# Windowed attention and mixture of experts on one core: the product with v as two runs of equal shapes, with constants, router groups and gate products moved

## The chip, the core and the metric

The kernel runs on one core of a Trainium2 chip. The core has a matrix engine (TensorE; PE in the profile, PEld for its weight loads), a vector engine (VectorE, DVE), an activation engine (ScalarE, ACT), a general engine (GpSimd, POOL) and a queue engine (SyncE, SP) that here only issues transfers. The engines run on their own and wait for one another through semaphores. Sixteen DMA engines carry the transfers of all queues. The metric is the device time of one execution in microseconds; the median of the runs shown stands for a kernel.

## The reference

Two stages, cut to what is computed. The first is causal attention with a window of 64 positions, for 8 batches, 8 heads, 576 positions and head size 64; the second sends each of the 4608 rows that passes a skip test to the best of 8 experts.

```python
scores = np.matmul(q, k.transpose(0, 1, 3, 2)) / np.sqrt(D)
rel = pos[:, None] - pos[None, :]
scores = np.where((rel >= 0) & (rel < 64), scores, -1e9)
attn = np.exp(scores - scores.max(-1)); attn /= attn.sum(-1) + 1e-9
x = (attn @ v)                                   # 4608 rows of 512
do_compute = x @ w_skip > 0
xc = x[do_compute]; logits = xc @ w_gate; e_idx = argmax(logits)
gate_w = softmax(logits)[e_idx]
h = np.maximum(xc[e_idx == e] @ w1[e], 0)        # per expert e
out[do_compute] = xc + gate_w * (h @ w2[e])
```

## The kernel before, in words

**Attention tiles.** A block is 64 positions of one batch. A tile `t` holds two blocks, 128 rows of x; there are 36. In 32 of them the two blocks follow each other in one batch; in the other four (tiles 8, 17, 26 and 35) they are the last blocks of two batches. A block attends to itself and to the block ahead of it, so a tile of the first kind needs three blocks of k and v, and the middle one is shared by both halves.

**One tile, step by step.** `score` (L244) writes the raw scores of a tile to `ps` in PSUM. `soften` selects the window (DVE, L260), takes the row maximum (DVE, L263), scales it (ACT, L264) and takes eight exponentials into `s` (ACT, L267). `transpose_p` turns `s` over on PE into two buffers `pt` (L276); ACT copies the first to `pm` (L283, L287), POOL multiplies that with the mask into `ptm` (L284, L288), and DVE does the rest of the mask (L291, the function that `transpose_p` returns and the loop calls as `masks`). `gate` and `gate_t` make the router's products with v ahead of time: `pw` on PE (L326), its copy `vw` on ACT (L328), `pk` on PE (L339), and the copy of that into columns 65 to 73 of `vm` on ACT (L340). `pt`, `pw`, `pk` and later `px` and `p1` share one tag `t` of two PSUM buffers in rotation. `av_tile` multiplies `ptm` with `vm` on PE into `av` (L376, one buffer), and DVE divides by the row sums into `x` and `lh` (L386 to L394).

**The product with v.** Four pairs of heads `q` and two halves `z` of the partitions give, for a tile with a shared block, eight products of 64 rows by 128 columns of weights (the middle block, for both halves of the tile at once) and sixteen of 64 by 64. The program writes 24 matmuls; the chip runs each float32 matmul as two instructions, so the profile counts 48 for a tile. The loop stands over `q`, and inside it come first the products of the shared block and then the others of the same `q`.

**The order of the work.** The instructions of every engine stand in the order in which the program issues them. Step `t` of the loop at the end of the program issues `score(t + 1)`, the gate products, `transpose_p(t)`, a step of the router, `soften(t + 1)`, loads, `masks`, `tile_out(t - 1)` (that is `av_tile`) and more router steps.

**The router.** `GRP` cuts the 36 tiles into groups. When the last tile of a group is out, `route` starts for the group: a generator of some 16 small DVE instructions (L421 to L482), an exponential on ACT, and sums on PE (L449, L452) that go into a free part of `av`. Each call of `routes(1)` runs it to its next `yield`. Its results are list entries, one POOL scatter for each tile (`scatter`, L528), of which `pace(1)` issues one. When 22 tiles are out (`NCLOSE`), the lists of the two fullest experts are closed (`close_first`), read back (`first_lists`, `es`), and four gathers fetch the first expert rows (`gather_x`, L551, `xg`). In steps `XSPLIT` the first two of them are turned over on PE into `px` (L739). In steps `U0` one 512 KB load of expert weights each is issued (`weight_dma_first`); in a step of `USPLIT` the first piece is split into a high and a low part (`weight_split`: ACT L702, DVE L703).

**The experts.** Behind the loop the last two tiles are interleaved with expert work (`p`, L750 to L752, and so on), which fills the rest of the program.

**Constants.** Nine small loads stand on ACT's queue ahead of its first instruction; the last three are those of `load_constants`.

## Time and profile before

| | |
|---|---|
| three runs | 497.98, 493.5 and 498.54 us, median 497.98 |
| the profiled execution | 500.87 us; span from its first to its last instruction 499.2 us |
| busy share of the span | PE 90%, PEld 73%, DVE 57%, ACT 42%, POOL 36% |
| first product with v (tile 0) starts | 19.96 us |
| product of tile 14 starts | 88.12 us |
| product of tile 34 starts, and first expert matmul | 219.49 us, 223.87 us |
| mean granted TensorE clock | 0.934 of full speed |

Busy PE is not PE at its peak: matmuls overlap in the engine, and their ends are modelled. How long a stage takes is read from the starts of its instructions. [...]

### The profile page before, as it was taken

How to read it: one execution, taken by the hardware profiler on the slowest of the kernel's cores; microseconds unless marked ns; L12 is line 12 of the kernel's file. 1: busy time of each engine (PE TensorE's matmuls, PEld its weight loads, DVE VectorE, ACT ScalarE, POOL GpSimd, SP SyncE). 2: the span in 40 equal slices, each digit the busy share in tenths (PEclk: the TensorE clock that was granted, in tenths of full speed). 3: DMA queues.
4: the chain of work that ended last, by engine and by line, in shares of the span. 5: the costliest groups of instructions: out<-in, count | busy, mean ns of one | idle time of the engine just before them, and what ended most of it. 6: DMA issues, size and time to landing. Idle time of an engine off the chain costs nothing.

```text
span 499.2 us, 12731 instructions
## 1 busy us (share of the span) xinstructions
PE 451.2 (90%) x5001; PEld 365.7 (73%) x5001; DVE 283.0 (57%) x600; ACT 211.3 (42%) x604; POOL 178.5 (36%) x213
## 2 busy tenths in 40 slices
PE   3999999899988994988798999999999999999990
PEld 3677767666765773767797988898888889888770
DVE  2356665665666664457963364967437456666420
ACT  1665665444434452334731252443424435543410
POOL 4343443344644546336525351420604313101010
PEclk9999999898977897668899999999999999999996
DMA  8879998868877698316743455364645655656000
GB/s 306 334 226 298 301 298 256 313 176 275 224 257 213 181 356 301 110 44 201 260 121 142 165 186 167 121 245 149 205 161 173 204 180 183 224 194 207 3 26 18
DMA packets 34958, 99.90 MB, mean 200 GB/s; under 512 B 6092, under 2 KB 7910, under 8 KB 34888
## 3 DMA queue, kind: packets, MB, share of 16 engines
q1 hardware_dynamic: 28864, 88.52, 54.5%
q0 software_dynamic: 4864, 9.90, 5.9%
q8 instruction: 40, 0.66, 0.5%
q10 hardware_dynamic: 1168, 0.65, 0.4%
q14 instruction: 22, 0.18, 0.1%
HBM read 84.82 MB, written 14.94 MB: 200 GB/s over the span
## 4 chain that ended last, share of the span: by engine, by line
PE 76%; DVE 8%; DMA 6%; issue 3%; ACT 3%; another core or an unknown queue 0%; POOLq 0%; SPq 0%; ACTq 0%; DVEq 0%
PE av L376 17%; PE p L750 7%; PE p L751 7%; PE p L752 7%; PE ps L244 5%; PE pt L276 5%; PE yw L750 3%; PE yv L750 3%; PE yw L751 3%; PE yv L751 3%; PE yw L752 3%; PE yv L752 3%; DMA raw<-wq 3%; PE px L739 2%; PE pk L339 2%
## 5 line engine op out<-in xcount | busy, mean ns | idle before, releaser
L376 PE MATMUL av<-vm,ptm 64*64 64x74 f32 (+1 forms) x1536 | 101.5, 285 | 1.9 <-DVE lh L394 1.5
L703 DVE TENSOR_TENSOR wlo<-raw,whi 128x1024 fp32r<-128x1024 f32 x72 | 87.8, 1222 | 14.3 <-ACT whi L702 12.4
L376 PEld LDWEIGHTS av<-vm,ptm 64*64 64x64 f32 (+1 forms) x1536 | 75.2, 164 | 27.6 <-issue 9.3
L787 ACT ACTIVATE hh<-p 128x256 fp32r<-128x256 f32 (+6 forms) x72 | 27.7, 385 | 140.6 <-PE p L752 139.2
L750 PE MATMUL p<-xh,whi 128*128 128x256 f32 (+6 forms) x288 | 85.8, 298 | 1.1 <-DVE hl L788 1.1
L751 PE MATMUL p<-xl,whi 128*128 128x256 f32 (+6 forms) x288 | 84.7, 294 | 0.0
L752 PE MATMUL p<-xh,wlo 128*128 128x256 f32 (+6 forms) x288 | 84.5, 293 | 0.0
L702 ACT CAST whi<-raw 128x1024 fp32r<-128x1024 f32 x72 | 74.5, 1046 | 0.0
L284 POOL TENSOR_TENSOR ptm<-pm,mask 128x512 f32<-128x512 f32 x36 | 45.9, 1276 | 76.1 <-ACT pm L283 76.0
L788 DVE SCALAR_TENSOR_TENSOR hl<-p,hh 128x256 fp32r<-128x256 f32 (+6 forms) x72 | 30.3, 420 | 70.3 <-ACT hh L787 64.6
L267 ACT ACTIVATE s<-ps,nmx 128x64 f32<-128x64 f32 x288 | 63.0, 330 | 1.2
L810 POOL DMA_INDIRECT out<-yo,les x18 | 19.0, 1054 | 122.3 <-DVE yo L809 109.8
L750 PEld LDWEIGHTS p<-xh,whi 128*128 128x128 f32 x288 | 55.7, 193 | 4.0 <-DVE hl L788 1.2
L528 POOL DMA_INDIRECT lists<-ent,gdi x36 | 40.7, 1130 | 46.4 <-DVE lh L394 22.6
L751 PEld LDWEIGHTS p<-xl,whi 128*128 128x128 f32 x288 | 55.8, 194 | 1.4
L752 PEld LDWEIGHTS p<-xh,wlo 128*128 128x128 f32 x288 | 55.7, 194 | 0.0
L276 PE MATMUL pt<-ident,s 128*128 128x128 f32 x144 | 34.5, 328 | 13.1 <-ACT vw L328 6.3
L386 DVE TENSOR_SCALAR r<-av 128x8 f32<-128x8 f32 x36 | 6.0, 166 | 71.1 <-PE av L376 69.4
L244 PE MATMUL ps<-k,q 64*64 64x128 f32 (+1 forms) x1024 | 42.7, 295 | 0.8 <-issue 0.8
L276 PEld LDWEIGHTS pt<-ident,s 128*128 128x128 f32 x144 | 16.3, 153 | 30.7 <-ACT vw L328 11.3
L244 PEld LDWEIGHTS ps<-k,q 64*64 64x64 f32 x1024 | 34.8, 153 | 2.0 <-issue 1.8
L750 PE MATMUL yw<-whi,hh 128*128 128x512 f32 x80 | 32.3, 403 | 0.0
(171 smaller groups left out, 703.2 us busy)
## 6 DMA issues: line engine op xcount, KB each, us to landing
raw<-wq SPq DMA_DIRECT2D x72, 512.0 KB
vm<-vp SPq DMA_DIRECT2D x16, 592.0 KB
vT<-vT SPq DMA_DIRECT2D x16, 512.0 KB
out<-x SPq DMA_DIRECT2D x32, 256.0 KB
q<-qT SPq DMA_DIRECT2D x14, 512.0 KB
k<-kT SPq DMA_DIRECT2D x7, 640.0 KB
k<-kT SPq DMA_DIRECT2D x7, 512.0 KB
kt<-kT SPq DMA_DIRECT2D x8, 256.0 KB
```

What stands on the lines that cost most here:

```text
L244: nc.tensor.matmul(ps[64 * hf : 64 * hf + 64, z, p, 64 * w.start :], q[h, p], k[h, w, p], start=True, stop=True, skip_group_check=True,)
L267: nc.scalar.activation(s[:, q, z], cur[:, z, q], AF.Exp, bias=nmx[:, z, q : q + 1], scale=0.125)
L276: nc.tensor.transpose(pt[:, i], s[:, 2 * g + i].rearrange("p z c -> p (z c)"), ident)
L284: nc.gpsimd.tensor_tensor(part(0, 2), split(pm[:, 0:2], 2), kept(2), op=ALU.mult)
L376: nc.tensor.matmul(av[64 * f0 : 64 * f1, z, q * VW : (q + 1) * VW], ptm[h, q, j : j + f1 - f0], v[h, q], start=first, stop=not first or (f ...
L528: ins = nc.gpsimd.indirect_dma_start(out=lists, out_offset=bass.IndirectOffsetOnAxis(ap=di, axis=0), in_=ent.bitcast(I32), in_offset=None, ...
L702: nc.scalar.copy(hi, raw)
L703: nc.vector.tensor_tensor(lo, raw, hi.bitcast(F32), op=ALU.subtract)
L750: nc.tensor.matmul(o, lh, rh, start=first, stop=False)
L751: nc.tensor.matmul(o, lh, rl, start=False, stop=False)
L752: nc.tensor.matmul(o, ll, rh, start=False, stop=last)
L788: beat(nc.vector.scalar_tensor_tensor(hl[:, f], p1, 0.0, hh[:, f].bitcast(F32), op0=ALU.max, op1=ALU.subtract))
```

## The change

The product with v loops over the shapes first and over `q` inside: all products of the shared block, then all others; the flags that open and close the sums follow that. In a tile without a shared block both kinds are 64 by 64. The gate products stand behind the transposes of the same step. The router's steps stand behind `soften` and the first feed of loads, ahead of `masks` and behind it. `GRP` has six groups instead of five: 8, 8, 6, 8, 4 and 2 tiles. `load_constants` moves from ACT's queue to SP's and into step 1 of the loop, ACT's other loads are put in another order, and `onesb` gets its ones early, followed by one exponential of zero times itself (its values stay one). `U0`, `USPLIT`, `XSPLIT` and `TWICE` go up by one; the loop ends with step 34, so that no step of it is in `USPLIT` any more.

```diff
-U0 = (28, 29, 30, 31, 32, 33)
-USPLIT = (34,)
+U0 = (29, 30, 31, 32, 33, 34)
+USPLIT = (35,)
-XSPLIT = (32, 33)
+XSPLIT = (33, 34)
-TWICE = 20
+TWICE = 21
...
     def load_constants():
-        nc.scalar.dma_start(cf, a["c_f"])
-        nc.scalar.dma_start(trib, a["c_tri"])
-        nc.scalar.dma_start(
+        nc.sync.dma_start(cf, a["c_f"])
+        nc.sync.dma_start(trib, a["c_tri"])
+        nc.sync.dma_start(
...
-        nc.gpsimd.memset(onesb, 1.0)
         nc.gpsimd.tensor_copy(base, cf[:, off["base"]])
...
-        for q in range(4):
-            parts = [] if shared else [(hf, hf + 1, 2 * hf + 1, win[hf][0], True) for hf in range(2)]
-            if shared:
-                parts.append((0, 2, 1, win[0][0], True))
-            parts += [
-                (0, 1, 0, win[0][1], False),
-                (1, 2, 3 if shared else 2, win[1][0] if shared else win[1][1], False),
-            ]
-            for n, (f0, f1, j, v, first) in enumerate(parts):
...
+        if shared:
+            both = [(0, 2, 1, win[0][0])]
+            rest = [(0, 1, 0, win[0][1]), (1, 2, 3, win[1][0])]
+        else:
+            both = [(hf, hf + 1, 2 * hf + 1, win[hf][0]) for hf in range(2)]
+            rest = [(hf, hf + 1, 2 * hf, win[hf][1]) for hf in range(2)]
+        for parts in (both, rest):
+            for q in range(4):
+                for f0, f1, j, v in parts:
...
-    GRP = [14, 8, 8, 4, 2]
+    GRP = [8, 8, 6, 8, 4, 2]
...
         load_qk(0, 0, 2)
+        nc.scalar.dma_start(band, a["c_band"])
         nc.scalar.dma_start(identb, a["c_identb"])
-        nc.scalar.dma_start(band, a["c_band"])
         nc.scalar.dma_start(sel, a["c_sel"])
+        nc.scalar.dma_start(wg, a["wg"])
         nc.scalar.dma_start(ident, a["c_ident"])
         nc.scalar.dma_start(mask, a["c_mask"])
-        nc.scalar.dma_start(wg, a["wg"])
+        nc.gpsimd.memset(onesb, 1.0)
+        nc.scalar.activation(onesb, onesb, AF.Exp, scale=0.0)
...
-        load_constants()
...
             score(t + 1)
+            masks = transpose_p(t)
             for f, n in gate_at.get(t, ()):
                 f(n)
-            masks = transpose_p(t)
             rest = its[0].split(*xhl[0], XSPLIT.index(t), "t") if t in XSPLIT else None
-            routes(1)
             soften(t + 1)
             pace(1)
             feed(t, 0)
+            if t == 1:
+                load_constants()
+            routes(1)
             masks()
+            routes(1)
             if t >= 1:
                 tile_out(t - 1)
...
             if rest is not None:
                 rest()
-            routes(1)
             routes(1 if t < NCLOSE - 1 else 2)
```

On PE, step 2 of the loop stands so before; `ps` are scores, `pk` a gate product, `pt` transposes and `av` the product of tile 1:

```order
L244 MATMUL ps<-k_108,q 64x128 x16
L339 MATMUL pk<-ident,vw_301 64x64 x8
L276 MATMUL pt<-ident,s 128x128 x4
L376 MATMUL av<-vm,ptm 128x74 x2
L376 MATMUL av<-vm,ptm 64x74 x4
L376 MATMUL av<-vm,ptm 128x74 x2
L376 MATMUL av<-vm,ptm 64x74 x4
L376 MATMUL av<-vm,ptm 128x74 x2
L376 MATMUL av<-vm,ptm 64x74 x4
L376 MATMUL av<-vm,ptm 128x74 x2
L376 MATMUL av<-vm,ptm 64x74 x4
```

The eight runs of the product become two, and the gate product stands behind the transposes. The same step on PE, after:

```order
L243 MATMUL ps<-k_108,q 64x128 x16
L275 MATMUL pt<-ident,s 128x128 x4
L338 MATMUL pk<-ident,vw_310 64x64 x8
L375 MATMUL av<-vm,ptm 128x74 x8
L375 MATMUL av<-vm,ptm 64x74 x16
```

The number of matmuls is the same; the row length that order prints first is that of the output's partitions.

On DVE, the first router group ends before with tile 13; its steps stand there between that tile's `lh` and the window (`ps`) and maximum (`mx`) of tile 16, in one piece:

```order
L394 TENSOR_TENSOR lh<-av,r 128x8x9
L421 TENSOR_REDUCE lg<-lh 128x126
L428 TENSOR_REDUCE gmx<-lg 128x14
L430 TENSOR_TENSOR gd<-lg,gmx 128x112
L433 SCALAR_TENSOR_TENSOR gfi<-gd,cf 128x112
L435 TENSOR_REDUCE gfm<-gfi 128x14
L260 COPY_PREDICATED ps<-sel,ps 128x8x64
L263 TENSOR_REDUCE mx<-ps 128x8
```

The first group now ends with tile 7, and on DVE its steps stand so:

```order
L393 TENSOR_TENSOR lh<-av,r 128x8x9
L420 TENSOR_REDUCE lg<-lh 128x72
L259 COPY_PREDICATED ps<-sel,ps 128x8x64
L262 TENSOR_REDUCE mx<-ps 128x8
L427 TENSOR_REDUCE gmx<-lg 128x8
L429 TENSOR_TENSOR gd<-lg,gmx 128x64
L290 TENSOR_TENSOR ptm<-pt,mask 128x256
L432 SCALAR_TENSOR_TENSOR gfi<-gd,cf 128x64
L434 TENSOR_REDUCE gfm<-gfi 128x8
```

One router instruction instead of five stands ahead of the next tile's window and maximum, and the rest behind them.

On POOL, the four gathers of the first expert rows stand before among the mask products (`ptm`) of tiles 31 and 32; `es` are the list entries they go by:

```order
L607 TENSOR_TENSOR es_115<-es_115,ok_116 128x4
L608 TENSOR_TENSOR es_115<-es_115,ok_116 128x4
L551 DMA xg_117<-out,es_115 128x512
L284 TENSOR_TENSOR ptm<-pm,mask 128x512
L288 TENSOR_TENSOR ptm<-pm,mask 128x256
L551 DMA xg_118<-out,es_115 128x512
L551 DMA xg_119<-out,es_115 128x512
L284 TENSOR_TENSOR ptm<-pm,mask 128x512
L288 TENSOR_TENSOR ptm<-pm,mask 128x256
L551 DMA xg_120<-out,es_115 128x512
```

The first gather stands there behind the mask product of tile 30, and PE turns its rows over in step 32. After, the mask products in the piece are those of tiles 29 and 30:

```order
L606 TENSOR_TENSOR es_115<-es_115,ok_116 128x4
L607 TENSOR_TENSOR es_115<-es_115,ok_116 128x4
L283 TENSOR_TENSOR ptm<-pm,mask 128x512
L287 TENSOR_TENSOR ptm<-pm,mask 128x256
L550 DMA xg_117<-out,es_115 128x512
L550 DMA xg_118<-out,es_115 128x512
L283 TENSOR_TENSOR ptm<-pm,mask 128x512
L287 TENSOR_TENSOR ptm<-pm,mask 128x256
L550 DMA xg_119<-out,es_115 128x512
L550 DMA xg_120<-out,es_115 128x512
```

The first gather stands behind the mask product of tile 29, and PE turns its rows over in step 33.

## Rows read from the trace of the kernel before

**Rows 1.** The page: busy time, share of the span and instructions of each engine; and the granted TensorE clock in 40 slices of the span, in tenths.

```profile
PE 451.2 (90%) x5001; PEld 365.7 (73%) x5001; DVE 283.0 (57%) x600; ACT 211.3 (42%) x604; POOL 178.5 (36%) x213
...
PEclk9999999898977897668899999999999999999996
```

**Rows 2.** Busy time of each engine in four stretches: from the product of tile 0 to that of tile 14, from there to that of tile 34, the handover to the experts, and the experts. Columns: stretch, its length, busy time and instructions of each engine, granted clock, busy share of the DMA engines, GB/s.

```profile
19.96:88.12 68.16, 66.84 (x1311) 49.56 (x1310) 40.35 (x97) 40.47 (x169) 27.37 (x28) 1.00 0.87 276
88.12:219.49 131.37, 113.46 (x1902) 84.20 (x1902) 78.57 (x212) 57.36 (x237) 63.56 (x68) 0.83 0.72 228
219.49:260.00 40.51, 35.72 (x299) 31.86 (x300) 32.54 (x86) 17.84 (x29) 19.07 (x19) 0.85 0.53 170
260.00:499.20 239.20, 223.79 (x1355) 192.29 (x1353) 127.00 (x200) 88.68 (x145) 61.23 (x80) 0.98 0.47 157
```

**Rows 3.** PE in order of time: the first product with v, one whole tile of the quiet stretch, tile 14, and the handover to the experts. Columns: start, length, engine, line, what, count, idle time before it.

```profile
19.96 2.78 PE L376 MATMUL av<-vm,ptm 64*128 64x74 f32 x30
...
32.48 1.05 PE L244 MATMUL ps<-k,q 64*64 64x128 f32 x32
33.35 0.64 PE L339 MATMUL pk<-ident,vw 64*64 64x64 f32 x16
33.92 0.88 PE L276 MATMUL pt<-ident,s 128*128 128x128 f32 x4
34.74 2.73 PE L376 MATMUL av<-vm,ptm 64*128 64x74 f32 x48
...
88.12 2.73 PE L376 MATMUL av<-vm,ptm 64*128 64x74 f32 x48
...
219.49 4.45 PE L376 MATMUL av<-vm,ptm 64*128 64x74 f32 x48 [1.53 <-DVE lh L394]
223.87 0.58 PE L750 MATMUL p<-xh,whi 128*128 128x256 f32 x1
```

**Rows 4.** PE in order of time, in short windows inside the product of tile 2 (a shared block; the first two instructions of a pair of heads, the second two, the first four 64-by-64 ones, and the second two of the next pair) and of tile 8 (no shared block).

```profile
29.92 0.34 PE L376 MATMUL av<-vm,ptm 64*128 64x74 f32 x2
30.09 0.28 PE L376 MATMUL av<-vm,ptm 64*128 64x74 f32 x2
30.30 0.29 PE L376 MATMUL av<-vm,ptm 64*64 64x74 f32 x4
30.76 0.28 PE L376 MATMUL av<-vm,ptm 64*128 64x74 f32 x2
...
59.33 0.36 PE L376 MATMUL av<-vt,ptm 64*64 64x74 f32 x8
59.51 0.31 PE L376 MATMUL av<-vm,ptm 64*64 64x74 f32 x8
59.63 0.31 PE L376 MATMUL av<-vt,ptm 64*64 64x74 f32 x8
```

**Rows 5.** The start, in order of time: the first row maximum on DVE, the first gate product on PE with its wait for a constant, ACT's table load, the first exponentials, and the first transpose on PE.

```profile
7.70 0.69 DVE L263 TENSOR_REDUCE mx<-ps 128x8 f32<-128x512 f32 x1
...
10.04 1.08 PE L326 MATMUL pw<-vT,wg 128*32 128x256 f32 x8 [1.42 <-DMA wg<-wg]
10.78 1.28 ACT L264 ACT_TABLE_LOAD   x1 [10.78 <-DMA cf<-c_f]
...
12.31 1.75 ACT L267 ACTIVATE s<-ps,nmx 128x64 f32<-128x64 f32 x8
12.88 0.48 PE L276 MATMUL pt<-ident,s 128*128 128x128 f32 x1 [1.76 <-ACT s L267]
```

**Rows 6.** A quiet tile, in order of time: DVE takes up a finished product, and the exponentials of the scores that PE makes meanwhile.

```profile
66.44 0.17 DVE L386 TENSOR_SCALAR r<-av 128x8 f32<-128x8 f32 x1 [1.83 <-PE av L376]
...
69.35 1.75 ACT L267 ACTIVATE s<-ps,nmx 128x64 f32<-128x64 f32 x8
```

**Rows 7.** The end of the first router group, in order of time: the first of its instructions on DVE, the window of the next tile behind them, ACT's wait for the maximum, and the products of the two tiles after that on PE.

```profile
87.45 1.20 DVE L421 TENSOR_REDUCE lg<-lh 128x126 f32<-128x1008 f32 x1
...
90.62 0.69 DVE L260 COPY_PREDICATED ps<-sel,ps 128x512 f32<-128x512 int32 x1
...
92.06 0.21 ACT L264 ACTIVATE nmx<-mx 128x8 f32<-128x8 f32 x1 [3.57 <-DVE mx L263]
...
95.29 4.35 PE L376 MATMUL av<-vm,ptm 64*128 64x74 f32 x48
...
103.44 2.73 PE L376 MATMUL av<-vm,ptm 64*128 64x74 f32 x48
```

**Rows 8.** The first gather of expert rows, as POOL issues it, and the transposes on PE that wait for it.

```profile
191.51 1.10 POOL L551 DMA_INDIRECT xg<-out,es  x1 [0.92 <-DMA qt<-qT]
...
197.65 1.09 PE L739 MATMUL px<-ident,xg 128*128 128x128 f32 x4 [5.76 <-DMA xg<-out,es]
```

**Rows 9.** Two of the stretches at half clock (columns as in rows 2).

```profile
95.43:102.26 6.83, 6.83 (x90) 4.72 (x90) 2.59 (x12) 1.92 (x9) 1.70 (x4) 0.50 0.73 267
194.41:208.07 13.66, 10.35 (x101) 8.35 (x101) 4.15 (x16) 3.37 (x13) 6.66 (x9) 0.50 0.53 182
```

**Rows 10.** The first splits of expert weights: two high parts on ACT, and the first low part on DVE.

```profile
216.16 2.04 ACT L702 CAST whi<-raw 128x1024 fp32r<-128x1024 f32 x2
...
220.64 1.22 DVE L703 TENSOR_TENSOR wlo<-raw,whi 128x1024 fp32r<-128x1024 f32 x1
```

**Rows 11.** The stretch in which the loads of the start fill the DMA engines (columns as in rows 2).

```profile
5.00:20.00 15.00, 11.22 (x140) 7.58 (x138) 4.59 (x7) 6.94 (x25) 2.96 (x7) 1.00 1.02 381
```

## The prediction, made before the result was known

> **What bounds the kernel now.** I read the page's first part and the clock line, then a table by stage, then PE in order of time, and last what stands around PE's waits. PE is busy for 90% of the span [rows 1], so the question is what of that is work. The table [rows 2] cuts the span: 20 us of start, 68 us for 14 tiles, 131 us for the next 20, 40 us of handover, 239 us of experts. Nothing that the change edits runs in the last stage (223.79 of 239.20 us busy at a clock of 0.98), so I leave it alone.

> In the quiet stretch a tile takes 68.16 / 14 = 4.87 us, and PE has next to no gap. Per tile the others are busy for 40.35 / 14 = 2.88 us (DVE), 2.89 (ACT) and 1.96 (POOL), and the DMA engines for 0.87 x 4.87 = 4.24 us, at 276 GB/s, which is 1.34 MB a tile [rows 2]. PE is the bound, and 2.7 us of its 4.87 are the product with v [rows 3].

> Inside that product the time goes to something other than arithmetic. A pair of heads takes 30.76 - 30.09 = 0.67 us: 0.17 from the first two 64-by-128 instructions to the second two, 0.21 from there to the first 64-by-64 ones, and 0.29 for these and the way back [rows 4]. In tile 8, where all instructions are 64 by 64, a batch of eight follows the one ahead of it after 0.12 to 0.13 us, and only the first batch takes 0.18 [rows 4]. So a run of one shape settles at 0.065 us for four instructions, its first step costs 0.05 more, and the turns between shapes cost the rest. That the second product adds onto the first in PSUM isn't the price: in tile 8 it does so too.

> In the later stretch 20 tiles take 131.37 us, 34 more than 20 x 4.87. There PE waits, and the clock falls to half behind the waits: 0.83 on average [rows 2].

> **The product with v.** Before, a shared tile is 4 x 0.67 = 2.67 us. After, it is one run of eight 64-by-128 passes, a turn, and one run of eight 64-by-64 passes. The unknown is how closely 64-by-128 passes follow when they no longer stop. The first step is 0.17; in the 64-by-64 run the later steps are 0.05 shorter than the first, and I take the same: 0.12. That gives 0.17 + 6 x 0.12 = 0.89, the turn 0.21, the second run 0.115 + 6 x 0.065 = 0.51, and the way out 0.17: 1.78 us, **0.89 us less**. Bounds: if no step gets shorter, 7 x 0.17 + 0.21 + 7 x 0.115 + 0.17 = 2.38 (0.29 less); if the wide passes follow as closely as the narrow ones, 1.45 (1.22 less). No loss is possible from the same instructions with fewer turns, save through other engines. Tiles 8, 17, 26 and 35 gain nothing, but they are short already.

> [...]

> So a quiet tile is 4.87 - 0.89 = **3.98 us** of PE. Then other things come close. DMA: 1.34 MB at the 381 GB/s of the start [rows 11] is 3.5 us; at 276 / 0.87 = 317 GB/s it is 4.2. The loop through softening: from DVE's taking up of a product to the end of the exponentials of the scores made behind it are 71.10 - 66.44 = 4.66 us [rows 6]; the transposes that need them come a tile later, so two tiles must hold those 4.66 us, half the transposes (0.44), the gate product (0.6) and one product with v (1.8): 7.5 us, or 3.75 a tile. DVE and ACT at 2.9 are further off. I take 3.98.

> **The gate products behind the transposes** cost nothing: the same work in another place, with the copy of `pt` (0.4 us on ACT) covered by the second transposes; if that cover goes, some 0.3 us a tile come back. They also take away waits of the transposes for the copy of the gate product, which I leave out.

> **The router.** At the end of the first group its five instructions hold DVE from 87.45 to 90.62, ACT waits 3.57 us, and PE starts tile 15 7.2 us after tile 14 and tile 16 another 8.15 later, at half clock [rows 3, 7]. Now one instruction, for 8 tiles instead of 14, stands ahead of the next window. There is one group more, but each step holds at most 1.6 us of such work, which fits into DVE's 3.98 - 2.88 = 1.1 us of slack but for half a microsecond. The same holds for the closing of the lists in steps 25 to 28. Of the 34 us of excess I give 17 us to these bursts and the slow clock behind them, and leave 6.

> **The gathers.** The first gather is issued at 191.51, and PE waits 5.76 us for it [rows 8], after which the clock stays at half until 208.07 [rows 9]. Now the gather stands two steps further ahead of its transposes, and a tile ahead of where it stood: at 4 us a tile, 12 us or more for a transfer of 6. That wait goes, with the slow clock about 10 us; the two sets of transposes (1.1 us each) stay.

> What remains of the 34 us: 6 for bursts, 2 for the transposes, 4 for stalls that I see no edit for, and 4 for DMA, since 3 MB of weights now have to come within six tiles that are each 0.9 us shorter. That makes **16 us**.

> **The start.** The three loads of `load_constants` keep ACT from its table load until 10.78; that takes 1.28 us, and exponentials start at 12.31, though the maximum was there at 8.39 [rows 5]. Without those loads, and with the table loaded early, they start near 8.7. What is late next are the last of ACT's other constants (the sixth, then `wg`, was waited for until 10.04 [rows 5]; now it is `mask`, with `ident` ahead of it) and PE's own work for the first two tiles, so that of the 3.6 us I count **2.5**; between 1 and 3.6. `cf` and the lists move to SP's queue; behind them wait loads of step 1 (`q`, `vT`), needed four tiles later.

> **The handover.** No split of a weight piece is left in the loop. Before, the first low part is done by 221.9, and expert matmuls start as soon as tile 34 is out [rows 3, 10]. Now it stands on DVE behind the division of tile 34 (1.35 us) and takes 1.22: **2.6 us** of PE waiting. Between 1.2 (only DVE's work) and 4.

> **Sum**, against the profiled execution (500.87 us). From the product of tile 0 to that of tile 34: before 199.5 us; after 34 x 3.98 + 16 = 151.3: 48.2 less. Start 2.5 less, the product of tile 34 itself (4.4 at half clock) 1.5 less, handover 2.6 more: 49.6 less, 451.3 us. The profiled execution lies 2.9 us above the median of the runs, so the forecast is **449 us**.

> **Rivals.** (a) Another engine takes over: DMA or softening holds a tile at 4.4 us, and stalls stay at 25. Then 34 x 4.4 + 25 = 174.6, 25 less instead of 48: 472 us. For it: DMA's 0.87 share and both bounds within 0.5 us. Against: at the start the same engines carry 381 GB/s [rows 11].
> (b) The change doesn't do what it says: passes of one shape don't close up (0.29 a tile). Then 34 x 4.58 + 16 = 171.7, 28 less from there: 470 us; with nothing at all from the product, 480. Against: tile 8.
> (c) Slower: the clock. It fell whenever PE waited: behind the router at 95.43, during the wait for the gather at 194.41 [rows 9]; at half clock tile 15 took 103.44 - 95.29 = 8.15 us [rows 7], and with the shorter product 4.35 x 0.89 / 2.67 = 1.45 less, 6.7. A PE that waits in every tile could stay there. Before, a tile took 199.5 / 34 = 5.87 on average; it decides from (5.87 - 3.98) / (6.7 - 3.98) = 69% of the tiles at half clock. At 85% a tile is 6.3: 214, 15 us more, 512 us. [...] Against: at 3.98 us a tile PE is still the last to finish, and in the quiet stretch, with no gaps, the clock stayed at 1.00 [rows 2].

> **How the numbers follow.** The forecast's own case (435 to 462) has 0.70, (a) 0.15, (b) 0.07, (c) 0.04; 0.04 is left for things unseen on either side. The price of the product (0.29 to 1.22 less) is the widest term: at its best end, 34 x 0.33 = 11 us below, tempered by DMA and softening; at the other, (b). The range 432 to 476 holds the forecast's case, (a) and most of (b). Within 1%, which is what a measurement here can tell from no change, lies little of any case: faster 0.93, same 0.03, slower 0.04.

> **What would show it.** In the profile after: the product of a shared tile at 1.5 to 1.9 us at full clock, in two runs; quiet tiles of 3.8 to 4.3 us; no wait of `px` for a gather; the first product at 17 to 18 us; tile 34 at 165 to 175 us; expert matmuls some 2.6 us behind tile 34; and the same 239 us from there on. Wrong it would be if quiet tiles stayed above 4.5 us with PE idle in each, or if the clock were at half for most of the tiles.

## The result, and the profile after

The changed kernel takes **480.33 us** (median of four runs, 475.93 to 483.10), the kernel before beside it 496.56: a ratio of 0.965, with an interval of 0.954 to 0.976. Forecast were 449 us, with a range of 432 to 476. The direction holds, about a third of the gain came, and the time lies outside the range. The profiled execution took 482.33 us. Medians here are of all runs, while ratios and their intervals leave out the runs that lie over 1.5% above the fastest of the same kernel.

The page after: busy times, the granted clock in 40 slices, and the queue of PE's instruction blocks (packets, MB, share of 16 engines).

```profile
PE 417.6 (87%) x5002; PEld 348.7 (73%) x5002; DVE 285.9 (59%) x616; ACT 209.8 (44%) x607; POOL 176.5 (37%) x216
...
PEclk9989999989797978979999999999999999999996
...
q8 instruction: 40, 0.66, 0.5%
```

The stages (columns as in [rows 2]): the start, 14 tiles, the next 20, the handover, the experts; and then tile 0 to tile 34 in one row.

```profile
0.00:15.43 15.43, 9.20 (x139) 6.20 (x139) 5.01 (x8) 7.11 (x26) 8.60 (x20) 1.00 0.87 300
15.43:83.79 68.36, 58.08 (x1323) 46.01 (x1319) 42.75 (x113) 39.15 (x170) 32.01 (x36) 0.98 0.91 311
83.79:200.45 116.66, 92.69 (x1897) 73.66 (x1894) 78.06 (x210) 56.12 (x237) 56.80 (x63) 0.88 0.79 254
200.45:241.00 40.55, 33.39 (x295) 30.15 (x296) 33.03 (x87) 18.84 (x30) 17.71 (x20) 0.87 0.50 163
241.00:480.60 239.60, 224.26 (x1359) 192.70 (x1357) 127.04 (x200) 88.56 (x145) 61.42 (x80) 0.98 0.48 158
...
15.43:200.45 185.02, 150.78 (x3216) 119.67 (x3213) 120.81 (x322) 95.27 (x407) 88.81 (x98) 0.92 0.83 275
```

Set the last row beside [rows 2]. PE's busy time from tile 0 to tile 34 was 66.84 + 113.46 = 180.3 us and is now 150.8: **29.5 us less**, as the prediction had it for the product (the product's row was 2.73 us [rows 3] and is 1.80; 31 shared tiles of 0.93 us are 29). But the stretch shrank only from 199.5 to 185.0. PE's idle time rose from 19.2 to 34.2 us. The first 14 tiles, which were quiet before, take 68.36 us, as long as before, with 10.3 us of idle in place of 1.3. The start is 4.5 us shorter; from tile 34 to the end nothing changed in this pair (279.7 and 280.1 us).

PE in order of time: a gate product and the product of a quiet tile, as in [rows 3], and two short windows inside that product, as in [rows 4].

```profile
83.18 0.68 PE L338 MATMUL pk<-ident,vw 64*64 64x64 f32 x16 [0.30 <-ACT pm L282]
83.79 1.80 PE L375 MATMUL av<-vm,ptm 64*128 64x74 f32 x48
...
84.18 0.39 PE L375 MATMUL av<-vm,ptm 64*128 64x74 f32 x4
84.30 0.39 PE L375 MATMUL av<-vm,ptm 64*128 64x74 f32 x4
```

The product itself is 1.80 us (predicted 1.78); pairs of 64-by-128 instructions follow each other after 0.11 us (predicted 0.12). What PE waits for from tile 0 to tile 34 (line, releaser, us in total, times, longest), the two largest waits of the kernel before ahead of those of the changed kernel:

```profile
PE px L739 <- DMA xg<-out,es: 5.8, 1, 5.8
PE pt L276 <- ACT vw L328: 5.7, 5, 2.1
```

```profile
PE pk L338 <- DVE ptm L290: 7.1, 4, 3.8
PE av L375 <- POOL ptm L283: 6.0, 2, 3.1
PE pw L325 <- ACT pm L282: 5.6, 13, 2.1
PE pk L338 <- ACT pm L282: 3.5, 10, 1.1
PE px L738 <- DVE ptm L290: 2.8, 1, 2.8
PE ps L243 <- issue: 2.1, 7, 0.4
PE pw L325 <- issue: 1.5, 2, 1.2
```

The gate products, `pw` and `pk`, wait 7.1 + 5.6 + 3.5 = **16.2 us** for `pm` and the masks (with the 1.5 us of `issue`, the 17.7 that an expectation below names). In two further executions of the changed kernel these are 13.9 and 13.6 us. They share two banks with the transposes (tag "t"). Behind the transposes they must wait until ACT has copied the first bank away (`pm`), 0.3 us most times; and where a step holds two gate products, the second takes the other bank, which DVE frees only with the masks. That is the long kind:

PE and DVE in order of time, between the products of tiles 24 and 25, and the stretch at half clock that begins there (columns as in [rows 2]).

```profile
141.18 0.64 PE L325 MATMUL pw<-vT,wg 128*32 128x256 f32 x8
145.58 0.69 PE L338 MATMUL pk<-ident,vw 64*64 64x64 f32 x8 [3.76 <-DVE ptm L290]
...
142.47 0.68 DVE L259 COPY_PREDICATED ps<-sel,ps 128x512 f32<-128x512 int32 x1
143.19 0.69 DVE L262 TENSOR_REDUCE mx<-ps 128x8 f32<-128x512 f32 x1
143.80 0.92 DVE L581 SCALAR_TENSOR_TENSOR ct<-cf,first 128x8 f32<-128x8 f32 x1
144.84 0.68 DVE L290 TENSOR_TENSOR ptm<-pt,mask 128x512 f32<-128x512 f32 x1
...
145.12:151.94 6.82, 6.36 (x92) 5.57 (x92) 3.03 (x13) 2.21 (x11) 1.70 (x2) 0.50 0.40 122
```

DVE reaches the masks (144.84) only behind the next window and a router piece of 0.92 us; PE stands for 3.76 us, until 145.58, and from 145.12 on the granted clock is 0.50 for 6.8 us. The second new wait is on POOL:

```profile
159.22 1.00 POOL L527 DMA_INDIRECT lists<-ent,gdi  x1 [0.17 <-DVE r L385]
166.28 0.60 POOL L617 DMA_DIRECT2D es<-lists  x1 [6.05 <-DMA lists<-ent,gdi]
168.06 1.27 POOL L283 TENSOR_TENSOR ptm<-pm,mask 128x512 f32<-128x512 f32 x1
...
169.39 2.94 PE L375 MATMUL av<-vm,ptm 64*128 64x74 f32 x39 [3.10 <-POOL ptm L283]
```

POOL waits 6.05 us for the last scatter to land before it reads a list, and the masks of the next tile queue behind that. The other of PE's waits for POOL's masks (2.85 us, in tile 2) stands behind the copy of `base`, which waits 10.2 us on POOL for `cf` from SP's queue.

### The profile page after: what moved, and what is told of

Its sections match the earlier page's. It is cut to its first block, busy times and chain, and to the rows that moved or that the text cites. A ratio compares the mean times of both kernels' runs of the same rounds, so it can differ in the third digit from the quotient of the medians.

```text
span 480.6 us, 12788 instructions
## 1 busy us (share of the span) xinstructions
PE 417.6 (87%) x5002; PEld 348.7 (73%) x5002; DVE 285.9 (59%) x616; ACT 209.8 (44%) x607; POOL 176.5 (37%) x216
## 4 chain that ended last, share of the span: by engine, by line
PE 72%; DVE 10%; issue 6%; ACT 4%; DMA 4%; POOL 1%; POOLq 0%; another core or an unknown queue 0%; ACTq 0%; DVEq 0%; SPq 0%
PE av L375 12%; PE p L749 7%; PE p L751 7%; PE p L750 7%; PE ps L243 6%; PE yw L749 3%; PE yv L749 3%; PE yw L750 3%; PE yv L751 3%; PE yv L750 3%; PE yw L751 3%; PE pt L275 2%; DVE wlo L702 2%; PE pk L338 2%; PE px L738 2%
## 5 line engine op out<-in xcount | busy, mean ns | idle before, releaser
L375 PE MATMUL av<-vm,ptm 64*64 64x74 f32 (+1 forms) x1536 | 67.2, 262 | 8.9 <-POOL ptm L283 6.0
L375 PEld LDWEIGHTS av<-vm,ptm 64*64 64x64 f32 (+1 forms) x1536 | 58.4, 164 | 18.8 <-issue 7.6
L527 POOL DMA_INDIRECT lists<-ent,gdi x36 | 38.2, 1060 | 49.9 <-DVE lh L393 14.9
L243 PE MATMUL ps<-k,q 64*64 64x128 f32 (+1 forms) x1024 | 45.6, 296 | 2.8 <-issue 1.8
L243 PEld LDWEIGHTS ps<-k,q 64*64 64x64 f32 x1024 | 36.5, 153 | 5.8 <-issue 5.3
L282 ACT COPY pm<-pt 128x256 f32<-128x256 f32 x36 | 13.6, 378 | 47.8 <-PE pt L275 45.5
L259 DVE COPY_PREDICATED ps<-sel,ps 128x512 f32<-128x512 int32 x36 | 25.4, 707 | 11.9 <-PE ps L243 9.4
```

Of the source, the lines that this page charges most:

```text
L243: nc.tensor.matmul(ps[64 * hf : 64 * hf + 64, z, p, 64 * w.start :], q[h, p], k[h, w, p], start=True, stop=True, skip_group_check=True,)
L375: nc.tensor.matmul(av[64 * f0 : 64 * f1, z, q * VW : (q + 1) * VW], ptm[h, q, j : j + f1 - f0], v[h, q], start=q == 0 and parts is both, s ...
L527: ins = nc.gpsimd.indirect_dma_start(out=lists, out_offset=bass.IndirectOffsetOnAxis(ap=di, axis=0), in_=ent.bitcast(I32), in_offset=None, ...
```

## The experiments

Times are medians beside the kernel before, whose medians in the four groups of experiments were 487.85, 489.73, 485.94 and 486.80 us: within 0.8%, so that I also compare across groups, with as much doubt. "The stretch" is tile 0 to tile 34 of the profiled execution. One kernel's stretch differs by up to 10 us from one execution to the next (the kernel before 199.5 and 189.0, the changed kernel 185.0, 175.4 and 177.3, the last version here 166.0 and 171.9), so that a difference of a few microseconds between two stretches shows nothing by itself.

**The kernel before again, and the changed kernel again.** No edit.

> The kernel before, unchanged, for its trace beside these runs: the chips of the experiments gave it 487.85 and 489.73 us, not the 496.56 us that stood beside the changed kernel. If its stalls are its own, PE's busy time from the product of tile 0 to that of tile 34 is again near 180.3 us, and the stretch 190 to 200 us; if the chip differs in more than that, the gather's wait of 5.76 us or the long tiles 14, 15 and 30 are absent.

> The changed kernel itself once more, beside the kernels of this group, since the kernel before took 487.85 us beside the first group of experiments and 496.56 us beside the changed kernel. If the two chips differ by a factor alone: 0.960 to 0.970 of the kernel before, as measured before; then the place of the gates alone (0.9597) is worth half a per cent. If the changed kernel does worse here, 0.97 to 0.98, the gates are worth 1 to 2%.

> The changed kernel beside the version put together from the experiments, on one chip. From the group before: 0.970 to 0.983 of the kernel before.

Measured: the kernel before at 488.95 us; the changed kernel at 476.88 us beside 489.73 (0.983, 0.965 to 1.001) and at 475.07 beside 486.80 (**0.978**, 0.972 to 0.984). These are not the numbers of the first pair. Two rows of the kernel before (stretch, and the largest waits of PE in it), and then the changed kernel's stretch:

```profile
19.23:208.20 188.97, 176.20 (x3213) 130.89 (x3212) 121.28 (x308) 97.65 (x405) 90.92 (x96) 0.91 0.80 259
...
PE pt L276 <- ACT s L267: 2.7, 3, 1.2
PE pt L276 <- ACT vw L328: 1.9, 3, 0.8
```

```profile
16.67:192.02 175.35, 147.58 (x3215) 119.82 (x3213) 119.79 (x322) 95.44 (x406) 88.42 (x97) 0.91 0.86 287
```

The wait of 5.76 us for the gather [rows 8] is 0.7 us here. The 34 us of excess that the prediction worked with are 189.0 - 34 x 4.87 = 23 us in this execution: some 10 us of what I meant to gain are not there in it. Both kernels took longer in the first pair (496.56 and 480.33 us) than in the later groups; why stays open.

**The gates, undone and alone.** First undone in the changed kernel; then made alone in the kernel before.

```
-            masks = transpose_p(t)
             for f, n in gate_at.get(t, ()):
                 f(n)
+            masks = transpose_p(t)
```

> The changed kernel with one edit undone: the gate products stand ahead of the tile's transposes again, as before the change. In the changed kernel PE waits 5.6 us in pw and 3.5 us in pk for the copy pm, 7.1 us in pk for the masks on DVE and 1.5 us more in pw: 17.7 us that the prediction had put at nothing; in the kernel before, with the gates ahead, the transposes waited 6.5 us for the copies of the gate products. Theory A (the place of the gates ate the gain): these 17.7 us go, some 6 come back in the transposes, and with less of the slow clock the time falls from 480 to 464 to 472 us. Rival B (the loop through softening or the transfers set the pace, and the gates only wait where something else would): within 1% of the changed kernel, 476 to 485 us.

> The kernel before with one edit of the change alone: the gate products behind the tile's transposes. The prediction had this at nothing, and at 0.3 us a tile if the cover goes. Theory A (they wait for the copy pm and the masks, in whose banks they write): quiet tiles rise from 4.87 to some 5.05 us, 6 us in all, pk waits some 6 us more for masks behind the router's pieces, and 3 to 6 us of the transposes' waits for the copies of the gates go: 1 to 2.5% slower than the kernel before. Rival B (the cost is only there with the other edits): within 1% of it.

Alone, the edit costs **21 us**: 507.86 beside 486.80 (1.046, 1.039 to 1.053), where theory A expected 5 to 12. The stretch, and PE's waits in it:

```profile
18.87:227.55 208.68, 180.22 (x3215) 133.94 (x3212) 119.66 (x307) 95.71 (x405) 89.44 (x95) 0.87 0.74 237
...
PE pk L339 <- DVE ptm L291: 7.8, 3, 3.9
PE px L739 <- DMA xg<-out,es: 6.7, 1, 6.7
PE pk L339 <- ACT pm L283: 3.4, 12, 0.3
PE pw L326 <- ACT pm L283: 3.4, 12, 0.3
```

14.6 us of new waits at the gates, and a granted clock of 0.87 in place of 0.91. The wait for the gather (6.7 us) was not expected, and I can't say whether it belongs to the edit: the kernel before has it in one execution (5.8 us) and hardly in the other (0.7). Quiet tiles are 5.05 us there.

Undone in the changed kernel it gains less: 468.97 us, the median of three runs (a fourth took 1323.57), beside 487.85 (0.960, 0.956 to 0.963). That is 6 to 8 us below the changed kernel's two later medians, and 9 us by the ratio beside the closer of them (0.978). The 16.2 us are gone, and others have come:

```profile
16.42:188.03 171.61, 148.92 (x3214) 119.59 (x3213) 120.93 (x323) 98.19 (x407) 90.58 (x99) 0.90 0.88 293
...
PE ps L243 <- issue: 7.8, 5, 2.8
PE av L375 <- POOL ptm L283: 4.4, 1, 4.4
PE pw L325 <- issue: 1.8, 1, 1.8
```

"Issue" means that the profile shows nothing that PE waits for. But it shows what lands. Here PE stops in the middle of the scores of a tile, of whose 32 instructions the first 25 used the same loads:

```profile
57.99 0.70 PE L243 MATMUL ps<-k,q 64*64 64x128 f32 x7 [2.77 <-issue]
```

and between 55.6 and 56.7 us one packet stands on a queue of instructions that by its count of packets (below) is PE's, among data that take 89% of the DMA engines:

```profile
q1 hardware_dynamic: 71, 0.24, 89.4%
q8 instruction: 1, 0.02, 5.5%
```

It lands at 56.61; PE goes on 1.38 us later. Eight gaps of PE between 45 and 143 us, 11.4 us in all, end 1.25 to 1.52 us behind such a packet, which come every 6 to 7 us. The page has 40 packets with 0.66 MB, 16 KB each, for 2 x 5002 recorded instructions: some 250 to a packet. A tile issues some 190, so that 250 last 6.4 us at 4.87 us a tile and 5.2 us at 3.9.

A count settles that PE waits for these blocks. Up to the eight gaps the trace has 1473, 1729, 1985, 2753, 3265, 3777, 5057 and 5313 instructions of PE (matmuls, weight loads and those of its sequencer), each 193 more than a multiple of 256: PE stops at the same place of a block every time. Gaps of over 0.3 us at exactly this place, each of them ending 1.2 to 1.6 us behind a packet, are in the stretch of the other executions: with the old product one (0.5 us) and one (1.4 us) in the kernel before and none in `e4_old_product` and `g1_before_gates`; in the changed kernel, whose gates wait, one (0.7 us), four (4.4) and four (4.8); with the new product and the gates ahead, 5 to 11 in the kernels that load everything, 8 of them (11.1 us) in `e2_product_alone`.

The packets and the stops agree on the size of a block: some 250 instructions to one of 16 KB by the first, 256 by the second. At this pace, beside these loads, PE waits 11.4 us for them in this execution.

**The same in the best version.** The edit of the gates in the kernel put together at the end.

> The kernel g3_lists with the gate products behind the transposes. Theory A: pw and pk wait 14 to 17 us for pm and the masks; since tiles are slower, the waits that end behind a block of instructions fall from 6 us to less than 3; in sum 4 to 9 us longer than g3_lists. Rival B (one wait takes the place of the other, and the place of the gates is worth nothing): within 2 us of g3_lists.

Measured 477.53 us beside 465.46 for that kernel on the same chip: 0.981 against 0.957 with intervals apart (0.974 to 0.988 and 0.950 to 0.963), some 11 us. Theory A, at more than its price: one wait does not simply replace the other. Its waits are less than expected at the gates (12.5 us, for 14 to 17) and more behind blocks (5.8 us, for less than 3).

**The product, alone and undone.** The diff's new loop in the kernel before; the old loop in the changed kernel.

> The kernel before with the new order of the product with v and nothing else of the change. Theory A (the shorter product is worth its PE time where no new wait meets it): PE's busy time from tile 0 to tile 34 falls by 29 us, as it did in the changed kernel, and the time goes from 497 to 468 to 475 us, below the changed kernel. Rival B (any shorter tile only waits elsewhere, on transfers or softening): 480 to 488 us, with as many microseconds of PE idle as the changed kernel has, 34.

> The changed kernel with the product with v in the order of before. Theory A (the product carries the gain, and the other edits together are worth next to nothing): 493 to 502 us. Rival B (the product's gain is mostly waited away, and the start and the smaller groups bring what is seen): 483 to 490 us.

Alone: 472.59 us beside 487.85 (**0.966**, 0.964 to 0.968), 15 us. That lies in theory A's range of times, but the range was set from 497 us: of the 22 to 29 us that it stood for, 15 came. PE is busy 149.3 us in the stretch (176.2 before), and idle for 26.5 in place of 12.8: half of the gain is waited away, though with the gates ahead, and 11.1 of the 26.5 us stand at the ends of instruction blocks. Undone: 503.40 (1.028, 1.023 to 1.033), above both theories. So the rest of the change, without the product, makes the kernel some 14 us slower, and the product is worth some 27 us in its company. Its trace has no gap at the end of an instruction block, and a DMA share of 0.78, which fits a PE that is slow enough for both.

```profile
16.32:218.80 202.48, 179.62 (x3216) 134.76 (x3213) 122.30 (x322) 96.00 (x407) 88.84 (x98) 0.88 0.78 249
```

**Fewer bytes.** The kernel with the gates ahead, with most of `vT` left out (two tiles, zeroed once), and then also `q` and `k` of all groups beyond the first four. Their results are not those of the reference, and the stretch alone is read.

```
-        vT = vtp.tile([P, 4, 256], F32, name="vT")
+        vT = vTs[n % 2]
...
-        return nc.sync.dma_start(vT, a["vT"][n // 2, n % 2])
+        return nc.sync.dma_start(vT[:, :, 0:32], a["vT"][n // 2, n % 2, :, :, 0:32])
...
-                when_at(first_of[n] - AHEADQ, 0, load_k, n)
-                when_at(first_of[n] - AHEADQ, 1, load_q, n)
+                if n < 4:
+                    when_at(first_of[n] - AHEADQ, 0, load_k, n)
+                    when_at(first_of[n] - AHEADQ, 1, load_q, n)
```

> The kernel with the gates ahead of the transposes, with seven eighths of each load of vT left out (224 KB of some 1340 KB a tile; the rest of vT is zero, so gates are wrong and hardly any token is routed: only the stretch from the product of tile 0 to that of tile 34 is read, 171.6 us in the kernel that it is made from, of which the DMA engines were busy for 88%). Theory A (with the shorter product the transfers set the pace, and waits that show as issue in ps and pw are loads that come late): these waits, 12 us, go, with the slow clock behind them, and the stretch takes 148 to 158 us. Rival B (the waits come from DVE's and POOL's queues): 166 to 172 us.

> The kernel with the gates ahead of the transposes and seven eighths of each load of vT left out, and in addition the loads of q and k left out for all groups of tiles beyond the first four (later groups score the old q and k, so the output is wrong; only the stretch from tile 0 to tile 34 is read). Of some 1340 KB a tile about 580 are left. Theory A (the waits shown as issue end when a 16 KB block of PE's own instructions lands, 1.3 to 1.5 us ahead, and that block stands behind data on the DMA engines): of the 9 to 10 us of such waits less than 3 are left, and the stretch takes 150 to 160 us, against 171.6 and 166.6. Rival B (the blocks come late for a reason of their own, or the waits have another cause): these waits stay at 8 us or more, and the stretch at 164 us or more.

The two stretches, with PE's "issue" waits in them, to be read behind that of the kernel they are made from (171.61 us, DMA share 0.88, 293 GB/s):

```profile
15.60:182.21 166.61, 142.44 (x3214) 113.74 (x3213) 120.51 (x323) 97.13 (x406) 90.54 (x99) 0.95 0.83 261
...
PE av L379 <- issue: 3.8, 4, 2.4
PE ps L243 <- issue: 2.8, 3, 1.4
PE pw L329 <- issue: 2.5, 1, 2.5
```

```profile
16.57:172.92 156.35, 140.41 (x3214) 111.55 (x3213) 119.40 (x323) 98.47 (x407) 90.40 (x99) 0.96 0.62 191
...
PE pk L344 <- issue: 2.4, 1, 2.4
PE ps L245 <- issue: 1.8, 2, 1.1
```

With a seventh of the stretch's bytes gone (261 GB/s for 166.6 us against 293 for 171.6), 5 us go, no more than two executions of one kernel differ by, and 9 us of "issue" waits stay: rival B's side. With two fifths gone (191 GB/s for 156.4 us), 15 us go, more than that spread, and waits of 4.2 us are left (expected: under 3), the largest two shown above; three gaps at the end of a block, for eight, make 4.1 of them. So transfers hold some 15 of the 171.6 us: PE's idle time falls by 6.8 us (22.7 to 15.9), about as much as its gaps at block ends (7.3), and its busy time by 8.5, at a granted clock of 0.96 for 0.90. The late blocks fit as the cause of a good part of this; that they are all of it isn't shown, and the 15 us rest on one execution. That blocks stand in line behind data is what this speaks for, but they come late too with fewer bytes, and the packets themselves take no longer among more data (1.03 us on average in `e1_gate_ahead`, 1.14 in `e8_lighter`): what makes them late lies ahead of their start, and stays open.

**The tables.** In the kernel with the gates ahead, `U0`, `USPLIT`, `XSPLIT` and `TWICE` as before the change.

> The kernel with the gates ahead of the transposes (0.9597 of the kernel before) with, in addition, the four tables of steps as before the change (weight loads from step 28, one split of a weight piece in step 34, splits of x in steps 32 and 33, TWICE 20). Theory A (the handover costs what was predicted, since the first split stands behind the division of tile 34): expert matmuls start sooner, the product of tile 35 comes 7.5 us behind that of tile 34 instead of 11, and the time falls by 2 to 4 us, to 0.952 to 0.956. Rival B (the split in the loop delays the masks of tile 34, and the gathers wait again as before): 0.960 to 0.970.

466.43 us beside 489.73 (0.961, 0.944 to 0.978): the interval holds both theories, and `e1_gate_ahead` has 0.960, so the times don't settle it. The traces speak for theory A. The product of tile 35 comes 7.5 us behind that of tile 34, where it is 11.0 in `e1_gate_ahead`, both as expected. The stretch is the same (171.4), and from the product of tile 34 to the end are 466.7 - 187.3 = 279.4 us, where the changed kernel, on the same chip, needs 475.2 - 192.0 = 283.2. Over all kept executions that load everything, this end takes 277.0 to 279.7 us in the ten with `U0`, `USPLIT` and `TWICE` as before, and 280.1 to 283.4 in the six with the new ones. PE's wait for the first low part stands in the changed kernel's own trace:

```profile
204.77 0.58 PE L751 MATMUL p<-xh,wlo 128*128 128x256 f32 x1 [2.09 <-DVE wlo L702]
```

**The groups.** The kernel before with the new product, and

```
-    GRP = [14, 8, 8, 4, 2]
+    GRP = [8, 8, 6, 8, 4, 2]
```

> The kernel before with the new order of the product (0.9662 of the kernel before) and, in addition, the router groups of 8, 8, 6 tiles instead of 14, 8. Theory A (the burst behind tile 14 costs what was read from it): the 7.2 us of tile 14 and the slow tile behind it go, less one more burst at tiles 8 and 9 of at most 2 us: 4 to 8 us less, 0.950 to 0.958. Rival B (the bursts only move, or transfers hold the tiles): 0.963 to 0.970.

467.62 us beside 489.73 (0.968, 0.946 to 0.990), 5 us below the product alone by medians and not below it by ratios (0.966): by the times it is not settled. The stretch is 166.1 us in place of 175.8, but 4.5 us of that are a wait for the gather that stands in the trace of the product alone and not in this one, as it comes and goes in the kernel before. What the groups themselves did is seen at tile 14: the product of tile 15 starts 3.8 us behind it, where it was 7.2.

**The copy of `base`.** In the changed kernel, the copy in step 6 in place of step 1.

```
+    def copy_base():
         nc.gpsimd.tensor_copy(base, cf[:, off["base"]])
...
+            if t == 6:
+                copy_base()
```

> The changed kernel with the copy of base, which on POOL waits 10.2 us for cf in step 1 with the masks of tile 2 queued behind it, moved to step 6; the loads stay where they are. Theory A: the 2.85 us wait of the product in tile 2 goes, and with it the stretch of slow clock from 29.06 to 32.47 us, 4 to 5 us in all: 475 to 477 us. Rival B: the time is caught up later, where the transfers stand, and the end moves by less than 1.5 us.

475.77 us (0.972, 0.966 to 0.977), between the changed kernel's two later medians (476.88 and 475.07): rival B, although the time lies in theory A's range, which was set from 480 us. The wait in tile 2 is gone, but the changed kernel's second execution doesn't have it either, and its third has 1.6 us of it.

**The start.** The groups' kernel with the constants of the changed kernel, the early table load, and the copy of `base` in step 5.

> The kernel before with the new order of the product and the smaller groups (467.62 us, 0.955 by medians), and in addition the start of the changed kernel: constants in its order, the table load early, the constants of the router on SP's queue in step 1, with the copy of base in step 5, where nothing waits for it. Gates, tables and the places of the router's pieces stay as before the change. Theory A (the parts add up, and what cost time in the changed kernel were the gates behind the transposes, the moved tables and the copy of base): the first product comes at 15.5 to 16.5 us instead of 19.4, and the time is 2 to 4 us shorter, 0.945 to 0.952. Rival B (an earlier start only meets the loads sooner): 0.953 to 0.960.

467.41 us beside 485.94 (0.963, 0.950 to 0.975): as long as without, though the first product comes at 15.51 in place of 19.37. That is rival B's side: in the two traces the lead is gone by the product of tile 14 (85.77 and 86.27 us). What ate it is not settled.

**The lists.** That kernel, with

```
-            paced.extend([last_stores, first_lists, None, close_lists])
+            paced.extend([None, last_stores, first_lists, None, None, close_lists])
...
-XSPLIT = (32, 33)
+XSPLIT = (33, 34)
```

> The kernel e9_start with the first lists read half a tile later, their closing a whole tile later, and the splits of x in steps 33 and 34 as in the changed kernel. Theory A (POOL's wait of 4 to 6 us for a list to land holds the masks queued behind it, and PE waits 2.8 to 4.5 us for these in each kernel since the change): this wait falls below 1 us, with the slow clock behind it, and the time is 3 to 6 us shorter than e9_start. Rival B (the gathers now come too late for the splits of x, or the wait only moves to the next beat): within 2 us of e9_start, or longer.

> The kernel e10_lists once more (new order of the product, smaller groups, start of the changed kernel with the copy of base in step 5, gates ahead of the transposes, lists later): 0.950 to 0.960 of the kernel before, and 1.5 to 3% below the changed kernel on the same chip. If its lead over the changed kernel came from the chip, it is within 1% of it.

462.75 us beside 485.94 (0.957, 0.947 to 0.967), and again 465.46 beside 486.80 (**0.957**, 0.950 to 0.963), on the chip on which the changed kernel took 475.07 (0.978, 0.972 to 0.984). It beats the kernel before and the changed kernel. That it beats `e9_start` by 5 us is not settled, since two medians of itself lie 2.7 us apart and the intervals overlap; PE's wait for POOL's masks is 1.6 us in `e10_lists` and 0.8 in `g3_lists`, against 4.6 in `e9_start`, 2.8 in `e7_groups` and 4.4 in `e1_gate_ahead`.

## Why the prediction was wrong

**What failed, in the terms of the sum.** The stretch was to be 34 x 3.98 + 16 = 151.3 us, and is 185.0, 175.4 and 177.3 in three executions. The product came as forecast; the 16 us for stalls did not. Without the edit of the gates, which stood in the sum at nothing, the stretch is 171.6 and 171.4 us; with two fifths of the bytes gone as well, where the sum had 4 us for DMA, it is 156.4. So the gates hold 4 to 14 of the 24 to 34 us by which the stretch lies above the forecast, transfers some 15 of what is left without them, and some 5 stay open. (The sum itself gives 448.4 us, which was written down as 449.)

**The bound now, and the product with v: right.** A shared product is 1.80 us, and PE's busy time fell by 29.5 us. A quiet tile takes 3.9 us where the gates stand ahead (predicted 3.98) and 4.1 to 4.2 in the changed kernel. Eight of the shared tiles, the first ones of a batch, have 32 instructions and not 48, which the prediction didn't see; their products are as long and gain as much (2.68 to 1.78 us). The 2.38 us of the lower bound, in which no step between passes gets shorter, did not come: from one pair of wide passes to the next it is 0.11 us, where it was 0.17 [rows 4]. Rival (b) is out.

**The gates behind the transposes: the first step that failed.** I had them at nothing, with the copy "covered by the second transposes", and 0.3 us a tile "if that cover goes". The 0.3 us are there, in most tiles. What I did not see is which bank the second gate product takes: it waits for masks on DVE, behind the next window and the router's pieces, up to 3.8 us at a time, and 6.8 us at a granted clock of 0.50 begin at the end of that one. The waits of the transposes for the gates' copies, which I left out, were 6.5 us in one execution of the kernel before and 2.6 in the other, and are smaller than the 16.2 us. Alone the edit costs 21 us, in the changed kernel 6 to 9, in the best version some 11.

**Stalls and DMA: the second step that failed.** Predicted was a fall from 34 to 16 us; the stretch shows 185.0 - 34 x 3.98 = 50 (175.35 - 135.3 = 40 in its second execution). Of the terms: the burst of the router behind tile 14 did shrink with the groups (7.2 to 3.8 us), and the 11 us predicted for all of them are not settled; in the changed kernel their pieces hold the masks that `pk` waits for. The gather's wait is gone as predicted, though the kernel before hardly has it in another execution; the transposes `px` now wait 1.0 to 2.8 us for masks. "4 for DMA" was too little: some 15 us hang on transfers once the gates are out of the way. I looked at the bytes of the weights, and not at PE's own instructions, which wait up to 11.4 us at the ends of their blocks. In the changed kernel as it stands the gates slow PE down, and these gaps are 0.7 to 4.8 us: one wait hides a part of the other. The masks queued on POOL, behind its read of a list (3.1 to 4.4 us) and behind the copy of `base`, I had not priced at all: I named the loads that wait behind `cf` on SP's queue, and not who waits for `cf`.

**The start: more than predicted in place (4.5 us in the first pair, 2.6 to 3.4 by the later executions beside `b_before`; I had 2.5, at most 3.6), nothing seen in time**, by `e9_start`.

**The handover: right in kind.** Some 4 us for the moved tables, for 2.6 (bounds 1.2 to 4).

**Rivals.** (a), 472 us, was nearest in kind: it named transfers and stalls that stay, but it had neither the gates nor PE's instructions. By the number, the 480 us of "nothing at all from the product" in (b) was nearest, and that is luck, since the product gave what it should. (c) did not come: the clock of the stretch is 0.92, above the 0.89 that [rows 2] give together; nor did it fall behind every wait, as behind one of PE's of 1.22 us in the changed kernel, which ended at 78.91 and after which the granted clock was 1.00 up to 96.50. Neither sign of being wrong that the prediction named came either: quiet tiles did not stay above 4.5 us, and most of the loss lies outside them.

## What to carry to other kernels

When work is moved across a step that shares its banks, follow each bank to the engine that frees it, and price the whole queue ahead of the freeing instruction, not that instruction's own length. A term of a sum that is a stall seen once (here a 5.76 us wait for a gather) needs a second execution of the kernel before it is counted as a gain. An engine that gets through a tile in 3.9 us in place of 4.87 also uses up its instructions a quarter faster: look at its instruction packets when it waits for nothing, and count its instructions up to each stop.
